# Polysketch attention and a multiplicative FFN in one kernel: another order of the same instructions from the 61st step on

## The chip, the cores and the metric

One core of a Trainium2 chip runs the whole kernel in one launch. The metric is device time in microseconds (us), the median of several runs. The engines are TensorE (PE in the profile, its weight loads PEld), VectorE (DVE), ScalarE (ACT) and GpSimd (POOL); SyncE (SP) issues nearly all DMAs. What a matmul computes lies in PSUM, in eight banks, until another engine reads it.

## The reference

The attention is linear: each q and k row of 32 numbers becomes 64 features, the outer product of two sketches of 8.

```
def phi(x):                                   # S1, S2: 8 x 32
    a = einsum('rd,bhsd->bhsr', S1, x)
    b = einsum('rd,bhsd->bhsr', S2, x)
    return outer(a, b) per row                # 64 features
q_p, k_p = phi(q), phi(k)                     # q, k, v: 4 x 4 x 1088 x 32
kv = einsum('bhsf,bhsd->bhfd', k_p, v);  z = sum over s of k_p
x = (q_p @ kv) / (q_p @ z + 1e-6)             # then heads side by side: 4352 x 128
out = (((x @ w1) * (x @ w2)) @ w3) @ w_out    # w1, w2: 128 x 1024, w3: 1024 x 1024, w_out: 1024 x 128
```

S1, S2 and the weights are float64 and come as 64-bit words, which the kernel turns into float32 itself; q, k and v are float32.

## The kernel before

The work is written as 1,179 small named steps (`@step("k0.gram1")`), each one to a few dozen instructions. A string of all the names, ORDER, says in which order they are emitted, and the main loop ties each engine's instructions into that order, so each engine runs its own part of the list strictly in sequence. An instruction waits for its operands and for the buffer that it writes; nothing behind it on its engine may overtake it. ORDER is thus a schedule written out by hand or by a planner, and three more tables belong to it: SLOTS says which buffer (SBUF tile or PSUM bank) each tile of a kind gets, POOL names the steps that run on GpSimd rather than on VectorE, and CPV the copies that run on VectorE rather than on ScalarE. WARM gives the lengths of twelve steps of filler matmuls of zeros (`warm0` to `warm11`, L255), which keep TensorE going while there is no work.

The loads of inputs (steps that end in `.load`) go through SP in the same order. Their instructions also carry a wait that the main loop adds: a bulk load is issued only when the fourth bulk load before it has landed (`UNDER_WAY = 4`; the small kr0 and kr1 loads don't count).

Names of steps: the letter and number ahead of the point is the part of the work.

- `k0` to `k3`: keys and values of batch 0 to 3. `k0.max`, `k0.g`, `k0.lead` and `k0.rest` split k into a leading part and a rest (kk, L651). `k0.gram0` to `k0.gram4` sum the products of k with itself (L659, small matmuls of 32 columns of the array). From the sum follow `k0.Gm`, `Gt`, `Ga`, `Gb` (L217, L201, L204, L865), on PE `k0.T0`, `T1` (L883 to L891), then `N0`, `N1` (L912), on VectorE `Nb` (L937), which together scale the denominators. `k0.tr0`, `tr1` transpose k (L685), `kT0`, `kT1` copy that (L690), `ab0`, `ab1` are the sketches (L702), `kp0`, `kp1` the features (L677), `kv0` to `kv3` and `kvr` the product with v (L769, L776), `kzt` and `kqt` transpose kv (L789, L805). `kr0`, `kr1` are the 64 last rows of each sequence, two batches at a time (`kr1.tr`, L819).
- `q0`, `q1`: the queries of batch 0, 512 tokens each. `q0.C0`, `q0.C1`, `q1.C0` (L1030) and `q0.A1`, `q1.A0` (L1057, L1110) are sketches on PE; on VectorE `sm`, `st`, `sh`, `sl` (L1137, L201, L204, L1157) and `Ct` (L1130) split and sum them, `p01`, `p2`, `p12` (L1180, L1184), `dn`, `de`, `rc` (L1189, L1194, L1198) give the reciprocal denominators, `phi0` and `phi1` the features (L1208). `pt0`, `pt1` transpose them (L1228, L1246), `x0`, `x1` multiply with kv (L1267), `xc` copies (L1274), and `xT0`, `xT1` (L1291) write xT, the input of the FFN. `q2`, `q3`, `q4`, `q6` and `qr` do the same for more tokens.
- `w0`, `w1` and so on: an eighth of w1 and w2 or w3 or w_out each; `.load` (L430) brings raw words, `.c`, `.m`, `.j`, `.a` turn them into float32 on ACT, VectorE and GpSimd (L466 is `.j`). `f0` to `f7` fold w3 and w_out into one matrix w3o (L528 to L538).
- `g0` to `g3`: the FFN of the first 2,048 tokens, 512 at a time, in eight chunks of d_ff: `g0.4a` and `g0.4b` are x·w1 and x·w2 of chunk 4 (L1799, L1809, 128x512 matmuls, the bulk of the kernel), `c` a copy (L1804), `m` the product (L1815), `o` the last matmul (L1835). `h4` and `h6` are batches 2 and 3, with seven products in place of eight (L1673, L1759), `gr` the 256 last tokens; `st` steps store.

The first 27 us hold the loads and the chain from k0 and q0 to the first xT; from there TensorE has FFN matmuls between which the steps of later batches are strewn. The last stretch is gr and the stores.

The emitting loop is this, and nothing in it changes:

```
for name in ORDER.split():
    n = len(traced)
    steps.pop(name)()
    if name.endswith(".load") and name not in ("s.load", "kr0.load", "kr1.load"):
        bulk += [i for i in traced[n:] if i.engine == nc.sync.engine]
for ins, ahead in zip(bulk[UNDER_WAY:], bulk):
    tc.add_manual_dep(ins, ahead.name, landed, reason="under way")
```

Of the kernel before, what the change touches and what calls it, by code (L numbers as in the profile page):

```python
# [82 lines left out]
q0.al k0.Nf q0.phi0 q0.phi1 q0.A1 q0.smy w1.m1 k1.max q0.sty q0.shy k0.kv3 k0.kv1 k0.kv2 q0.sly s.KS k0.kvr kr1.tr
k0.kvm w1.m0 kr1.kT q0.p01 q1.C0 q1.C1 q0.C1 k0.kzt k2.loadr q0.pt0 q0.C1t q0.scy q0.p2 k0.kz q0.pt1 k0.kvc kr1.ab
k0.kqt q0.p12 q0.dn q0.de q0.rc w1.j0 q0.pc0 q0.pc1 q0.x0 k1.kT0 q0.x1 q0.xs0 q0.xs1 q0.xt0 w1.a0 q1.A0 k2.load
w0.load k1.lead0 q0.xc0 q0.xc1 k0.kq w1.a1 k2.max q0.xt1 k1.ab q0.xT0 q0.xT1 g0.4a q1.load g0.5a q1.sm w0.m1 q1.st
q1.Ct g0.4c g0.4b q1.sh q1.sl k1.rest0 g0.7b w0.c1 g0.7a k1.abt w0.j1 k1.gram0 w0.c0 s.RC q1.scy k1.gram1 kh2.load
q1.sca q2.tr g0.5c q1.al q1.p01 q1.p2 k1.gram2 k1.gram3 kr1.abc k1.gram4 w6.load w0.m0 g0.6b w0.j0 g0.7c g0.7m k1.Gm
q1.p12 k1.Gc g0.0a w2.load w0.a1 q1.dn q1.de q1.rc q1.bs k1.Gt g0.3a k1.Ga k1.T0 k2.kT1 k1.Gb g0.3c q1.restT g0.2a
q1.phi k1.T1 q1.pt0 g0.4m w0.a0 q2.max q2.l2 g0.6a k1.Ta k2.lead0 k2.rest0 g0.1a g0.2c k1.Tc g0.5b q3.tr g0.5m k1.Tb  # L90
q1.pc0 q1.pt1 g0.1b w9.load k1.N0 s.AR q2.l1 q2.rm v3.zero q1.pc1 k1.N1 q1.x g0.6c g0.1c k1.Na k1.Nr k3.zero k2.gram0
g0.1m k2.gram1 k2.gram2 q3.max k2.gram3 g0.0c k2.kT0 k1.Nb q1.xT k2.gram4 q3.l2 k2.ab q2.A0 q2.C0 q2.C1 q3.l1 k1.kp0
v1.zero w9.c k2.abt g1.5a g1.5c g1.1a q2.Ct g1.7a q2.At q3.rm q3.A0 k0.Nr q2.sm q3.C0 q3.C1 k2.Gm v1.loadr q2.st w2.m
q2.sh g1.1c g1.2a k1.kp1 g0.6m q3.Ct g1.0a g1.7b k3.load v1.load g1.5b q3.At k2.Gt k3.loadr w2.c k2.Ga g0.0b w9.j
q2.sl g1.7c w6.c g1.6a k1.kv0 q3.sm k2.Gb w5.load q2.sc q2.al g1.0c k2.Gc g1.7m q2.p01 q3.st k1.kv2 k1.kv3 q3.sh w9.m
k1.kv1 k2.T0 k1.kvr q3.sl q2.p2 k2.T1 q2.p12 q2.dn q2.de g1.4a q2.rc k3.max g0.3b g0.0m g1.1b kh3.load g1.4c k2.Ta
g1.2b q3.sc g1.2c w5.c k2.Tc k1.kvc k1.kqt k1.kq g0.3m q3.p01 g1.6c g1.3a g1.5m g1.3b q2.bs q2.phi0 q2.pT0 g1.2m g1.3c
q2.x q2.load k2.N0 k2.Tb k3.lead0 w9.a1 k2.N1 g1.4b q3.al q3.p2 q3.p12 q2.xT0 g2.5a k3.kT1 g2.5c g2.6a q3.dn q3.de
k2.Na g1.3m g2.4a g2.3a w5.m g2.4b g2.6c k3.rest0 g1.0b k2.Nr q3.rc g1.1m g1.4m g1.6b k2.Nb g0.2b kr1.kp w6.j q4.tr
g2.4c g1.6m w7.load w7.c q3.bs q4.max q2.restT w6.m w5.j w2.j q4.l2 w3.load w9.a0 k3.gram0 k3.gram1 k3.gram2 q3.load  # L100
w7.j q3.phi0 k3.gram3 k3.gram4 g2.2a k3.Gc g2.1a g1.0m w2.a0 g2.6b g2.0a g2.4m g2.1c f6.t w6.a0 w4.load g2.3b w2.a1
g2.2b g2.2c g2.0c w6.a1 g2.1b q3.pT0 k3.Gm g0.2m k3.Gt k3.kT0 v3.load w7.m f6.m w5.a1 w5.a0 g2.3c k3.Ga k3.Gb g2.3m
w7.a0 g2.1m w3.m g2.6m q3.x k3.T0 k3.T1 f2.t w3.c w3.j w8.load g2.0b q3.xT0 g3.1a f6.o k3.Ta g3.0a g3.0b g2.7a g2.7b
q4.l1 w7.a1 q4.rm g3.0c g3.0m g2.5b v3.loadr g3.3a w4.c g2.0m g2.2m g3.1c g2.5m g2.7c g2.7m v2.zero g3.6a k3.Tb
v2.loadr k3.ab f4.t k3.Tc k3.abt w4.j g3.3c w3.a1 q4.A0 q4.C0 q4.C1 q4.At k3.N0 k3.N1 v2.load w3.a0 f0.t k2.kp1 f4.m
w4.m g3.6c q3.restT q6.tr g3.6b g3.6m q4.Ct q4.sm w10.load f0.m k2.kp0 f4.o g3.1b f0.o g3.1m qr.max q6.max k3.kp1
q4.st k2.kv0 w4.a1 k3.kp0 k2.kv3 k2.kv1 k2.kv2 k2.kvr q4.sh qr.l2 k3.kv0 k3.kv1 f3.t k2.kvc k3.kv3 k3.kv2 k3.Na w4.a0
qr.l1 qr.rm q4.sl q4.sc q4.al k3.kvr k3.kvc g3.4a q6.l2 g3.4c g3.4b q4.p01 k3.Nr g3.3b q6.l1 w8.c g3.5a k3.Nb g2.4o
g3.4m f1.t f3.m w10.c k3.kqt g3.5c w8.m g3.3m q4.p2 q6.rm k3.kq f1.m f1.o q6.A0 q6.C0 w10.j q6.C1 g3.1o f3.o w8.j
q4.p12 q6.At g3.2b w10.m q6.Ct q4.dn g3.7a q6.sm q6.st w8.a0 w10.a0 qr.A0 qr.C0 qr.C1 g3.0o g2.1o g3.7c w10.a1 g0.3o  # L110
qr.Ct qr.At q6.sh q4.de g1.4o q4.rc q4.bs g3.5b q4.na w8.a1 f2.m f2.o q6.sl q6.sc g2.3o f7.t qr.sm g3.5m q4.nb q4.nm
# [1823 lines left out]
```

## Time and profile before

| | before |
|---|---|
| median of 3 runs | 245.04 us (244.92 to 245.08) |
| span of the profiled execution | 244.1 us, 0.94 less than the median |
| mean granted TensorE clock | 0.998 |
| TensorE busy | 236.2 us, 97% |
| VectorE, GpSimd, ScalarE busy | 206.7, 161.9, 123.5 us |
| TensorE's share of the chain of work that ended last | 87% |

The profile is one execution. A row of the timeline has the start and length in us, the engine, the line, the operation, out<-in and how many are grouped; in brackets stands the idle time before it and what ended it. "Issue" means that the engine waited for nothing that the profile shows. A row of the stretches has, for each engine, its busy us and the number of its instructions, then the granted clock, the share of the DMA engines' time and GB/s. Rows of one DMA line end with the time from issue to landing. Where matmuls overlap, their lengths sum to more than the time that they take.

### The profile page before, as it was taken

What the parts mean: (1) busy time and instruction counts of PE and PEld (TensorE: products, weight loads), DVE (VectorE), ACT (ScalarE), POOL (GpSimd) and SP (SyncE); (2) the same over time, 40 slices, a digit from 0 to 9 for tenths busy, and PEclk for the clock granted to TensorE, in tenths of its full rate; (3) what the DMA queues carried; (4) which work ended last, traced back from release to release, by engine and by line L of the source; (5) the groups of instructions that cost most, each with busy time, mean ns of one, the idle gap of its engine ahead of it and who ended that gap; (6) DMA issues with size and microseconds to landing.
All of it is one profiled execution on the core that took longest, in us unless ns stands there. A gap on an engine that the chain in (4) does not pass through costs nothing.

```text
span 244.1 us, 6745 instructions
## 1 busy us (share of the span) xinstructions
PE 236.2 (97%) x2724; PEld 129.8 (53%) x2724; DVE 206.7 (85%) x421; ACT 123.5 (51%) x246; POOL 161.9 (66%) x203
## 2 busy tenths in 40 slices
...
GB/s 201 265 143 325 181 227 190 6 197 224 220 141 251 188 217 190 59 1 3 3 0 0 4 0 3 59 113 3 1 0 0 0 3 0 0 1 3 12 90 93
DMA packets 31935, 22.06 MB, mean 90 GB/s; under 512 B 21280, under 2 KB 26528, under 8 KB 31904
## 3 DMA queue, kind: packets, MB, share of 16 engines
...
q8 instruction: 21, 0.34, 0.6%
q10 hardware_dynamic: 544, 0.52, 0.6%
q14 instruction: 10, 0.08, 0.1%
...
## 4 chain that ended last, share of the span: by engine, by line
PE 87%; DMA 5%; ACT 2%; POOL 2%; DVE 1%; issue 1%; POOLq 0%; SPq 0%
PE b_ps L1809 12%; PE ps_o L1835 12%; PE ps_X L1673 11%; PE a_ps L1799 11%; PE ps_o L1759 10%; PE ps_w3o L534 6%; PE ps_Y L1673 6%; PE ps_Z L1673 3%; PE ps_g L659 2%; PE ps_x L1527 2%; PE ps_ac L1374 2%; DMA qh<-in_q_dram 2%; DMA k<-in_k_dram 2%; PE ps_or L1824 2%; POOL ph L1208 1%; PE idle_ps L255 1%
## 5 line engine op out<-in xcount | busy, mean ns | idle before, releaser
L1673 PE MATMUL ps_X<-xd,wv 64*128 64x512 f32 x112 | 36.3, 593 | 0.0
L1799 PE MATMUL a_ps<-xT,w 128*128 128x512 f32 (+1 forms) x80 | 36.1, 562 | 0.0
L1809 PE MATMUL b_ps<-xT,w 128*128 128x512 f32 (+1 forms) x80 | 35.6, 555 | 0.0
L1804 ACT COPY ffa<-a_ps 128x512 f32<-128x512 f32 (+1 forms) x38 | 20.1, 540 | 29.2 <-PE a_ps L1799 26.7
L1707 POOL TENSOR_TENSOR hc<-hc 128x512 f32<-128x512 f32 x16 | 20.7, 1304 | 15.7 <-DVE hc L1685 15.5
L1835 PE MATMUL ps_o<-ab,w3o 128*128 128x512 f32 x64 | 29.6, 600 | 0.0
L1680 ACT COPY hc<-ps_X 128x512 f32<-128x512 f32 x38 | 21.3, 590 | 16.1 <-PE ps_X L1673 12.9
L1815 DVE TENSOR_TENSOR ab<-ffa,b_ps 128x512 f32<-128x512 f32 (+1 forms) x40 | 23.9, 623 | 4.9 <-PE b_ps L1809 4.1
L501 POOL TENSOR_TENSOR w3c<-w3c,cv_m 128x512 int32<-128x512 int32 x16 | 21.2, 1344 | 4.2 <-DVE w3c L495 4.1
L1673 PEld LDWEIGHTS ps_X<-xd,wv 64*128 64x128 f32 x112 | 14.9, 186 | 13.1 <-issue 10.9
L1799 PEld LDWEIGHTS a_ps<-xT,w 128*128 128x128 f32 x80 | 14.1, 189 | 13.9 <-issue 8.8
L1809 PEld LDWEIGHTS b_ps<-xT,w 128*128 128x128 f32 x80 | 14.4, 190 | 13.1 <-issue 8.1
L1673 PE MATMUL ps_Y<-xd,wv 64*128 64x512 f32 x48 | 19.7, 594 | 0.0
L1835 PEld LDWEIGHTS ps_o<-ab,w3o 128*128 128x128 f32 x64 | 11.6, 190 | 13.4 <-issue 13.0
L534 PEld LDWEIGHTS ps_w3o<-wo,w3T 128*128 128x128 f32 x128 | 15.3, 192 | 2.4 <-issue 2.4
L534 PE MATMUL ps_w3o<-wo,w3T 128*128 128x128 f32 x128 | 15.7, 276 | 0.0
L1759 PE MATMUL ps_o<-hc,w3o 128*64 128x512 f32 x32 | 15.1, 595 | 0.0
L1759 PE MATMUL ps_o<-tt,ws 128*64 128x512 f32 x32 | 13.7, 594 | 0.0
L1680 ACT COPY hc<-ps_Y 128x512 f32<-128x512 f32 x14 | 8.1, 592 | 9.7 <-PE ps_Y L1673 6.6
L263 ACT ACTIVATE cv_c<-raw 128x1024 f32<-128x1024 f32 (+1 forms) x13 | 13.0, 1014 | 0.0
L1540 ACT COPY xd<-ps_x 64x256 f32<-64x256 f32 x24 | 8.8, 367 | 7.2 <-PE ps_o L1835 6.8
...
## 6 DMA issues: line engine op xcount, KB each, us to landing
...
```

The costliest lines, as they stand in the source:

```text
L263: act.activation(dst, hi.bitcast(F32), ACT.Prelu, scale=2.0 ** -112, alpha=-2.0 ** 32)
L501: pool.tensor_tensor(d, d, x["m"][:, i * 512:(i + 1) * 512], ALU.add)
L534: pe.matmul(t["o"], w3T[ko][:, c], wo[:, c], start=c == 0, stop=c == NC - 1)
L1673: pe.matmul(x[bank], stat(j, u)[:, i * 128:(i + 1) * 128], rows(j, u), start=new, stop=True, tile_position=(u * 64, 0), skip_group_check=True)
L1680: cp(n(y))(x[k], x[bank])
L1707: on(f"h{g}.{i}m{k}").tensor_mul(both[0][k], both[0][k], both[1][k])
L1759: pe.matmul(acc_o[bank][half[0]:half[1]], w(i), x(i), start=n == 1, stop=n == (2 if j == 3 else 4), tile_position=(0, half[0]), skip_group ...
L1799: pe.matmul(x["a"][:, :w], w_of(0, c), xT[g][:, c0:c0 + w], start=True, stop=True)
L1804: cp(f"g{g}.{c}{su}c")(x["s"][:, :w], x["a"][:, :w])
L1809: pe.matmul(x["b"][:, :w], w_of(1, c), xT[g][:, c0:c0 + w], start=True, stop=True)
L1815: dve.tensor_mul(ab_sb[g, c][:, c0:c0 + w], x["s"][:, :w], x["b"][:, :w])
L1835: pe.matmul(o_ps[g], w3o[:, c], ab_sb[g, c], start=n == 1, stop=n == NC)
```

## The change

Only the tables change: SLOTS, POOL, CPV, and ORDER from its 61st name on. The steps are the same 1,179, WARM too. POOL has 91 names in place of 90 (32 left, 33 came in), CPV 26 in place of 17. Of the names that matter in the first 50 us, `q0.phi0`, `q0.p2`, `q0.p12` and `k2.lead0` move to GpSimd, and `k0.kp1`, `k0.Nf`, `s.KS`, `q1.phi` and `k2.rest0` from it to VectorE. In all VectorE has 376 steps in place of 365, ScalarE 192 in place of 204, GpSimd 138 in place of 137.

```
 CPV = set("""
-    g0.0c g0.1c h4.1ac h4.1ad h6.1bc h6.2ad k0.kT1 k1.kvc k2.kT1 k2.kq k3.kT0 k3.kT1 k3.kq q0.xc0
-    q0.xc1 q6.xT0 q6.xT2
+    g0.3c g0.6c g1.2c g2.0c g2.2c g2.4c g2.5c g3.2c g3.3c gr.5c h4.0ac h4.0bd h4.2be h4.3bc h6.0bd
+    h6.1ac h6.2be k0.kT1 k1.kT0 k1.kvc kr1.kT q0.xc0 q1.pc1 q4.xT2 q4.xT3 q6.xT3
 """.split())
...
-k1.zero s.Pm warm5 q0.l1 q0.A0 warm6 kr0.ab k0.lead1 q0.rm q0.sma q0.sta warm7 k0.kT0 v0.load v0.loadr k1.load k0.ab1
-q0.sha k0.rest1 q0.C0 k0.gram1 k0.gram2 k0.gram3 k0.gram4 k0.ab0 k0.abc1 q1.max q0.C0t q0.sla q1.l2 k1.loadr s.Pp
...
+k1.zero s.Pm warm5 q0.l1 q0.A0 warm6 kr0.ab k0.lead1 q0.rm q0.sma k0.ab1 k0.gram1 q0.C0 k0.kT0 q0.sta kr1.load q0.sha
+s.KS k0.rest1 kr1.tr k0.gram2 warm7 k0.abc1 k0.ab0 q0.sla w1.c0 k0.kp1 kr1.kT q1.max w0.load kr0.abc k1.loadr q0.C0t
...
```

**SP, the loads behind the first weights** (raw tiles are a quarter of w1 and w2; k_264, v_146 and so on are tiles; L572, L593 and L609 load the last rows). Before:

```order
L430 DMA raw_211<-in_moe_w1_dram 128x512
L430 DMA raw_211<-in_moe_w2_dram 128x512
L582 DMA v_146<-in_v_dram 128x4x256
L593 DMA v_146<-in_v_dram 64x4x32
L560 DMA k_264<-in_k_dram 128x4x256
L572 DMA k_264<-in_k_dram 64x4x32
L609 DMA kr1_436<-in_k_dram 64x4x32 x2
```

And now:

```order
L430 DMA raw_211<-in_moe_w1_dram 128x512
L430 DMA raw_211<-in_moe_w2_dram 128x512
L609 DMA kr1_328<-in_k_dram 64x4x32 x2
L430 DMA raw_373<-in_moe_w1_dram 128x512
L430 DMA raw_373<-in_moe_w2_dram 128x512
L572 DMA k_264<-in_k_dram 64x4x32
L560 DMA k_264<-in_k_dram 128x4x256
L582 DMA v_146<-in_v_dram 128x4x256
L593 DMA v_146<-in_v_dram 64x4x32
```

The second pair of weights (step w0, raw_373) and k of batch 1 (k_264) stand ahead of v of batch 0 (v_146), which stood right behind the first pair.

**VectorE, the end of the chain to the first xT** (s_rc are the reciprocals, xc the copies, xT the FFN's input). Before:

```order
L1189 TENSOR_REDUCE s_d_620<-s_pr_561 128x2x16
L1194 SCALAR_TENSOR_TENSOR s_rc_622<-s_d_620 128x16
L1198 RECIPROCAL s_rc_622<-s_rc_622 128x16
L466 TENSOR_SCALAR w12_81<-cv_c_402 128x2x256
L1274 COPY xc_656<-ps_xt_629 128x256
L1274 COPY xc_656<-ps_xt_634 128x256
L1291 TENSOR_TENSOR xT_686<-xc_656,ps_xs_640 128x256
L1291 TENSOR_TENSOR xT_686<-xc_656,ps_xs_665 128x256
```

And now:

```order
L204 SCALAR_TENSOR_TENSOR s_hl_611<-s_g_540,s_t2_574 128x2x128
L466 TENSOR_SCALAR w12_81<-cv_c_516 128x2x256
L1130 STREAM_TRANSPOSE ay_C_642<-ps_c_578 128x384
L1189 TENSOR_REDUCE s_d_644<-s_pr_605 128x2x16
L466 TENSOR_SCALAR w12_81<-cv_c_364 128x2x256
L1194 SCALAR_TENSOR_TENSOR s_rc_653<-s_d_644 128x16
L1198 RECIPROCAL s_rc_653<-s_rc_653 128x16
L1157 TENSOR_TENSOR s_hl_611<-ps_a_525,s_hl_611 128x2x128
L690 COPY kT_665<-ps_kt_452 128x512
L1274 COPY xc_673<-ps_xt_660 128x256
L1291 TENSOR_TENSOR xT_683<-xc_673,ps_xs_680 128x256
L1291 TENSOR_TENSOR xT_683<-xc_673,ps_xs_687 128x256
```

Steps of q1 (s_hl_611, ay_C_642), a copy of k1's transposed keys (L690) and weight steps (L466) now stand among q0's last steps; one of the two copies L1274 went to ScalarE.

**TensorE, the gram of batch 2** (ps_g_959 before, ps_g_893 now, its sum in PSUM). Before, it follows q1's x and runs through its 72 matmuls to k2.ab (L727); its first rows:

```order
L912 MATMUL ps_N_920<-T_p_885,P2s_80 32x8 x8
L1297 MATMUL ps_x_944<-pT_906,kz0_605 64x512 x2
L659 MATMUL ps_g_959<-kk_891 32x64
L659 MATMUL ps_g_959<-k_439,kk_891 32x32
L659 MATMUL ps_g_959<-kk_891 32x64
```

Now it begins earlier and is broken off twice; the first break is this:

```order
L659 MATMUL ps_g_893<-k_650,kk_848 32x32
L883 MATMUL ps_T_936<-RS_71,G_a_930 32x32
L889 MATMUL ps_T_936<-RS_71,G_a_930 32x32
L890 MATMUL ps_T_936<-RS_71,G_c_910 32x32
L891 MATMUL ps_T_936<-RS_71,G_b_938 32x32
L659 MATMUL ps_g_893<-kk_848 32x64
L659 MATMUL ps_g_893<-k_650,kk_848 32x32
```

The second break, ahead of k2.gram3, is some 70 rows of other matmuls, three of them bulk ones of g1 at its end; k1.T0, k1.T1 stand in the first one.

More of the change, by code (lines that the diff above doesn't have):

```diff
@@ L83 @@
[L83 to L111, printed above, removed]
-g3.2a qr.st g3.2c g1.6o q4.nr q4.ne q4.nn q4.phi0 g0.2o q6.al k2.kqt f5.t g3.2m f5.m f5.o q4.phi1 q4.pT0 g3.7b g3.7m
```

132 lines of the change are left out of this document (81 added, 51 removed).

## The prediction

> **What bounds the kernel now.** I read the page first: who is busy, and where.
>
> ```profile
> PE 236.2 (97%) x2724; PEld 129.8 (53%) x2724; DVE 206.7 (85%) x421; ACT 123.5 (51%) x246; POOL 161.9 (66%) x203
> q8 instruction: 21, 0.34, 0.6%
> ```
>
> TensorE (PE) is busy for 236.2 of 244.1 us, so an order of the same matmuls can give at most the 7.9 us in which it is idle. The busy time in stretches says where those are (per engine: busy us, instructions; then the granted clock, the DMA share and GB/s).
>
> ```profile
> 5.00:10.00 5.00, 4.72 (x73) 3.72 (x70) 4.35 (x14) 3.86 (x14) 1.12 (x4) 1.00 0.93 218
> 10.00:15.00 5.00, 4.59 (x168) 4.25 (x160) 3.20 (x10) 4.56 (x9) 4.76 (x9) 1.00 0.88 256
> 20.00:25.00 5.00, 4.65 (x117) 3.86 (x116) 3.31 (x10) 3.05 (x11) 2.32 (x3) 1.00 0.91 292
> 45.00:50.00 5.00, 3.84 (x186) 2.74 (x175) 4.62 (x13) 2.26 (x3) 2.62 (x5) 1.00 0.05 10
> 240.00:245.00 5.00, 0.56 (x6) 0.37 (x4) 0.29 (x1) 0.27 (x1) 0.00 (x0) 0.82 0.32 66
> ```
>
> Two kinds of idle time: small pieces in the first 30 us, and one large piece at 45 to 50 us. What is lost at the end is the last tokens' chain through VectorE and the last store. The waits of PE and the timeline name the pieces.
>
> ```profile
> PE ps_g L659 <- issue: 1.6, 2, 1.2
> PE ps_kv L769 <- issue: 0.9, 1, 0.9
> PE ps_xs L1287 <- ACT xs L1280: 0.3, 1, 0.3
> PE ps_ph L1246 <- POOL ph L1208: 0.2, 1, 0.2
> ```
> ```profile
> 14.27 0.22 PE L659 MATMUL ps_g<-k,kk 128*32 128x32 f32 x1 [0.41 <-issue]
> 14.78 1.10 PE L702 MATMUL ps_ab<-RS,kT 128*128 128x64 f32 x8
> 18.06 0.26 PE L769 MATMUL ps_kv<-kp,v 128*32 128x64 f32 x3
> 20.35 0.69 PE L769 MATMUL ps_kv<-kp,v 128*32 128x64 f32 x34 [0.91 <-issue]
> 21.14 0.33 PE L819 MATMUL ps_krt<-ident,kr 128*128 128x128 f32 x1
> 27.42 1.10 PE L1799 MATMUL a_ps<-xT,w 128*128 128x512 f32 x2
> 46.98 0.19 PE L659 MATMUL ps_g<-k,kk 128*32 128x32 f32 x1 [1.16 <-issue]
> ```
>
> Three gaps, 0.41, 0.91 and 1.16 us, wait for nothing that the profile shows. All three lie inside runs of small matmuls (the gram, L659, and kv, L769). At 27.42 the first bulk matmul starts, a = x·w1 of the first 512 tokens; from there PE is full but for the last two kinds of gap. So the time is: when the bulk starts, plus the gaps behind it, plus a fixed amount of matmul work. I take the three gaps for the fetch of instructions: 2724 + 2724 instructions over 21 packets of queue q8 are 259 a packet, and one such packet is 16 KB. Counts over the same length of time before a gap and elsewhere:
>
> ```profile
> 11.00:13.90 2.90, 2.86 (x118) 2.66 (x115) 2.31 (x7) 2.83 (x7) 2.66 (x5) 1.00 1.00 281
> 16.60:19.50 2.90, 2.84 (x82) 2.07 (x80) 2.42 (x9) 2.73 (x8) 2.12 (x4) 1.00 0.77 256
> 43.00:45.90 2.90, 2.83 (x158) 1.88 (x149) 2.83 (x8) 2.32 (x6) 0.57 (x4) 1.00 0.02 6
> 31.50:34.50 3.00, 3.00 (x148) 2.27 (x147) 2.57 (x7) 2.49 (x6) 0.89 (x2) 1.00 0.94 221
> ```
>
> Before two of the gaps PE ran 233 and 307 instructions in 2.9 us, about a packet's worth; before the middle one 162. But 295 in 3 us went by without a gap, at 31.5. So density alone doesn't decide; where the run falls in its packet must do so too. The reading is likely, not sure.
>
> **The change part by part.** It moves steps from the 61st on; the matmuls stay the same. I go by the two ends of the sum: the bulk's start, and the gaps behind it.
>
> *The bulk's start.* It waits for xT of the first 512 tokens on VectorE (DVE), the end of this chain:
>
> ```profile
> 14.91 0.19 DVE L217 TENSOR_REDUCE G_g<-ps_g 128x1 f32<-128x32 f32 x1 [1.35 <-PE ps_g L659]
> 18.96 0.16 DVE L937 TENSOR_TENSOR RC<-RC,ps_Nr 128x8 f32<-128x8 f32 x1 [0.41 <-PE ps_Nr L912]
> 23.20 0.32 DVE L1068 STREAM_TRANSPOSE ay_C<-ps_cy 128x128 f32<-128x128 f32 x1 [1.38 <-PE ps_cy L1030]
> 26.48 0.79 DVE L1291 TENSOR_TENSOR xT<-xc,ps_xs 128x256 f32<-128x256 f32 x2
> ```
>
> From 14.91 to 27.27 DVE spends 12.36 us, of which 0.41 and 1.38 are waits: 10.57 of work. What the change takes out of that stretch and puts into it is priced by these rows:
>
> ```profile
> 19.64 0.78 DVE L1208 TENSOR_TENSOR ph<-s_al,s_bs 128x512 f32<-128x512 f32 x1
> 23.88 0.29 DVE L1180 TENSOR_TENSOR s_pr<-s_al,s_loy 128x128 f32<-128x128 f32 x1
> 15.69 0.42 DVE L466 TENSOR_SCALAR w<-cv_c 128x512 int32<-128x512 int32 x1
> 27.19 0.42 DVE L1137 TENSOR_REDUCE s_g<-ps_a 128x32 f32<-128x256 f32 x1
> 27.98 0.57 DVE L1130 STREAM_TRANSPOSE ay_C<-ps_c 128x384 f32<-128x384 f32 x1
> 6.71 0.67 DVE L690 COPY kT<-ps_kt 128x512 f32<-128x512 f32 x1
> ```
>
> Out: q0.phi0 (0.78) and q0.p2, q0.p12 (0.29 each) go to GpSimd, −1.36. In: a third weight step L466 (+0.42), the second half-batch's sm, st, sh, sl (four like L1137, 4 × 0.42) and Ct (0.57), the copy k1.kT0 (0.67) and a small step of the normaliser (about 0.2 by its neighbours): +3.54. Work 10.57 − 1.36 + 3.54 = 12.75. The two old waits are covered by this new work, so the stretch is only 0.4 longer if nothing new is waited for. It also begins later: k0.ab0 (L702, 1.10, some 0.1 of it overlapped), kr1.tr (0.33, likewise) and a filler stand ahead of the last gram matmuls now, and the 0.41 gap there goes; about +0.9 (0.7 to 1.1). DVE has k0.kp1 and the row transposes ahead of that point, which the old wait of 1.35 covers. Together the bulk would start 1.3 us later.
>
> *Late loads.* On SP the first weights' second quarter (w0, 1.05 MB) and k1 now stand ahead of v0.
>
> ```profile
> 5.52 0.43 SPq L582 DMA_DIRECT2D v<-in_v_dram  x1
> ```
> ```profile
> DMA to landing us min/median/max: 5.3/5.3/5.3
> ```
> ```profile
> DMA to landing us min/median/max: 7.2/7.2/7.2
> ```
>
> The first landing row is the w1 pair's, whose second half was issued at 5.1 and so landed at 10.4; the next is v0's: 5.52 + 7.2 = 12.7. So 0.52 MB behind w1 took 2.3 us. Here transfers issued together came in the order of issue. Now w0 (twice that), k1 and v0 follow w1: 10.4 + 4 × 2.3 = 19.6; at the best rate of a stretch (292 GB/s at 20 to 25 us) 2.1 MB take 7.2 us, 17.6. A bulk load is also held until the fourth before it has landed, so up to 20.9. k0.kv0 wants v0 on PE at 18.06 + about 0.5 (the gram before it is later by 0.9, of which fewer fillers make up some), and behind it on PE stands k0.N1, whose result the DVE chain needs (it already waited 0.41 for it). So the wait for v0 holds the bulk: 0 to 2.3 us, I take 0.7, since part of it falls while DVE still has other work. [...]
>
> Bulk start: 27.42 + 0.4 + 0.9 + 0.7 = 29.4, **+2.0 us** (+0.9 to +3.4).
>
> *The gaps behind it.* k2's gram is no longer one run: k1.T0, k1.T1, then bulk matmuls stand between its steps. If the gap at 46.98 is a fetch, it goes: **−1.16** (0 to −1.16). The wait of 0.2 for q1's ph (L1208 on GpSimd) goes, as that step now runs on DVE: **−0.2**.
>
> *Shape changes.* Going between matmuls of different array tiles costs PE a little:
>
> ```profile
> 49.17 2.77 PE a_ps L1799 x6
> 55.04 2.58 PE b_ps L1809 x6
> ```
>
> The same six, once beside narrower tiles and once among their like: 0.19 for a pair of changes. The changed program has two such pairs fewer: **−0.3** (0 to −0.4).
>
> *New waits.* k2.gram0 now follows soon after k2.rest0 on DVE, which stands behind q1.phi and a gram step there; g0.1a waits for a weight step on GpSimd behind k2.lead0, moved there. Neither shows in the trace of before. From zero to one bulk group of 1.7 us; I take **+0.4**, nearer zero, as DVE works ahead of PE by a few steps in this stretch.
>
> *The rest.* Behind 60 us PE is full in the trace and stays so with any order that keeps its operands ready. DVE has eleven steps more, at the 0.4 to 0.8 us of the rows above 4 to 9 us, on top of 85% busy, which can cost a little in the last stage of products; the chain of the last tokens at the end keeps its steps. I take nothing for both (−0.3 to +0.8).
>
> Sum: +2.0 − 1.16 − 0.2 − 0.3 + 0.4 = +0.7 (0.74). The profiled span is 244.1 and the median of the runs 245.04, 0.94 more; so 245.7.
>
> **The rivals.**
>
> *v0 lands in time* (faster). If the loads move at the higher rate, v0 and k1 are there by 18.5 us; the bulk starts 1.3 later, the gap of 1.16 goes, no new wait comes: +1.3 − 1.16 − 0.2 − 0.3 = −0.4, so 245.04 − 0.4 = 244.6; with 0.5 more from a chain of DVE that overlaps as well as it does now, 244.1. For it: 292 GB/s in one stretch. Against: 218 to 256 in the stretches that count. It decides at a landing of 18.5 us.
>
> *The loads are later still, and the gram waits* (slower). v0 at 20.9, k2.gram0 behind DVE by 1 us: 245.7 + 1.0 + 0.6 = 247.3. For it: the hold of four under way. Against: PE has several steps to fill with ahead of kv0's users.
>
> *The gaps are not fetches and stay* (the change doesn't do what it says). Then the 1.16 comes again at some place: 246.9. The row at 31.5 with 295 instructions and no gap speaks for it; the packet count, and that the waits show no engine, speak against it. [...]
>
> **How the numbers follow.** A measurement of this kernel can tell about 0.2%, 0.49 us, from no change: same is 244.55 to 245.53. The forecast's case, 0.42, spreads over 244.9 to 246.6: slower 0.22, same 0.15, faster 0.05. Loads in time 0.32: faster 0.24, same 0.08. Later still 0.14, gaps stay 0.12, both slower (0.01 of the last the same). That makes faster 0.29, same 0.24, slower 0.47. The range of 8 in 10 reaches from 244.0, the loads in time with a shorter chain (and 0.1 for the scatter of the runs), to 247.3, the late loads: the likeliest case's own range is 244.9 to 246.6.
>
> **What would show it.** Right: no wait "issue" over 0.5 us on PE behind the bulk's start; the first L1799 at 29 to 30 us; a wait of L769 or L912 for the DMA of v, or DVE waiting for ps_Nr by more than 0.41; the bulk's later start still there at the end. Wrong: the first L1799 at 28 or earlier, a gap of about 1 us in k2's gram, or a new wait over 1 us behind 50 us.

## The result and the profile after

The changed kernel takes 255.07 us (median, 254.3 to 256.9), the kernel before 244.98 us beside it (244.91 to 245.08): a ratio of 1.043, 95% interval 1.039 to 1.047. I had forecast 245.7 us and a range of 244.0 to 247.3; the sign was the likeliest one, the size was not in reach of the range. The profiled execution has a span of 255.1 us and a mean granted clock of 0.984, since the clock fell twice in it (0.72 and 0.84 in two of the stretches below); it is the slowest of the four (256.9). The kernel was run and profiled once more (e11 below): span 253.4 us, clock 0.997, the same waits. The clock's share is kept apart in what follows. Two executions of 607 us (e5) and 1341 us (the kernel before, beside e9 to e11) are in none of the times.

The page of the changed kernel, busy time of each engine:

```profile
PE 242.9 (95%) x2724; PEld 137.9 (54%) x2724; DVE 222.8 (87%) x435; ACT 115.6 (45%) x231; POOL 162.7 (64%) x204
```

The same 2,724 matmuls keep TensorE busy for 6.7 us more, and VectorE is busy for 16.1 us more with 14 more instructions, 1.2 us apiece. Both numbers should make a reader suspicious: a busy engine is not always an engine at work. The stretches and the waits of TensorE say where to look.

```profile
35.00:40.00 5.00, 3.67 (x11) 1.41 (x8) 4.97 (x6) 3.90 (x7) 4.79 (x2) 1.00 0.66 162
40.00:45.00 5.00, 4.25 (x60) 2.58 (x64) 4.89 (x8) 2.00 (x5) 2.07 (x3) 0.72 0.79 188
90.00:95.00 5.00, 3.17 (x79) 2.33 (x79) 4.25 (x7) 1.79 (x7) 2.12 (x2) 0.84 0.86 237
```
```profile
PE a_ps L1799 <- POOL w L470: 2.1, 1, 2.1
PE ps_x L1527 <- DVE ab L1815: 1.8, 1, 1.8
PE ps_g L659 <- issue: 1.1, 2, 0.7
```

Between 35 and 40 us VectorE is busy for 4.97 us with six instructions, GpSimd for 4.79 us with two. The timeline of GpSimd in the two places, then that of VectorE, and last the same two operations on VectorE in the kernel before:

```profile
35.21 4.25 POOL L214 TENSOR_SCALAR kk<-k,k_g 128x1152 f32<-128x1152 f32 x1 [1.28 <-PE ps_g L659]
39.43 1.27 POOL L470 TENSOR_TENSOR w<-w,cv_m 128x512 int32<-128x512 int32 x1
...
86.90 1.94 POOL L677 TENSOR_TENSOR kp<-kabt 128x1024 f32<-128x1024 f32 x1
88.79 0.20 POOL L577 MEMSET v<- 64x128 f32 x1
88.95 1.27 POOL L501 TENSOR_TENSOR w3c<-w3c,cv_m 128x512 int32<-128x512 int32 x1
90.19 1.94 POOL L677 TENSOR_TENSOR kp<-kabt 128x1024 f32<-128x1024 f32 x1
```
```profile
35.41 3.84 DVE L1204 TENSOR_TENSOR s_bs<-ay_C,s_rc 128x128 f32<-128x128 f32 x1
...
86.92 0.19 DVE L201 SCALAR_TENSOR_TENSOR G_t<-G_g,ps_g 128x32 f32<-128x32 f32 x1
87.02 1.88 DVE L1815 TENSOR_TENSOR ab<-ffa,b_ps 128x512 f32<-128x512 f32 x3
88.81 3.36 DVE L204 SCALAR_TENSOR_TENSOR G_a<-G_g,G_t 128x32 f32<-128x32 f32 x1
92.10 0.67 DVE L1815 TENSOR_TENSOR ab<-ffa,b_ps 128x512 f32<-128x512 f32 x1
```
```profile
15.36 0.19 DVE L204 SCALAR_TENSOR_TENSOR G_a<-G_g,G_t 128x32 f32<-128x32 f32 x1
39.51 0.86 DVE L214 TENSOR_SCALAR kk<-k,k_g 128x1152 f32<-128x1152 f32 x1
```

L204 on 128x32 took 0.19 us in the kernel before, at 15.36. Here it takes 3.36 and ends at 92.17, with GpSimd's kp (90.19 + 1.94 = 92.13); L1204 ends at 39.25, 0.2 us ahead of the end of GpSimd's L214 (39.46), and takes 0.29 us in e2 (35.78), where no GpSimd instruction runs beside it. The reading is that they are not slow but stand waiting while GpSimd runs, and that the profile counts this as busy. Both read two tiles of SBUF. L201 and the three products L1815 ahead of L204, which read one input from PSUM, run beside GpSimd's other kp (86.90 to 88.84) and take 0.19 us and 1.88 us for three, as in the kernel before (L201 at most 0.19 us, L1815 0.68 at the median). So this is the picture, which the experiments put to the test: k2.lead0 takes 4.25 us on GpSimd (0.86 on VectorE before), w0.a0 stands behind it and TensorE waits 2.08 us for w0.a0; and VectorE's k3.Ga stands through three GpSimd instructions in a row, the products behind it come 3.2 us late, and TensorE's q3.x, which needs their PSUM banks, waits 1.83 us.

How much of VectorE's 16.1 us is standing can be estimated from the traces: against the fastest instruction of the same operation, tiles and shape, its instructions take 14.0 us too long in all in the kernel before and 22.4 in the changed one. So about half, 8.4 us, is standing; the rest would be steps that came over.

The start of the bulk, and v0, of which the prediction spoke most:

```profile
L582 SPq DMA_DIRECT2D v<-in_v_dram x1: 374/374/374, 11.9 to 11.9; - x1
DMA to landing us min/median/max: 6.7/6.7/6.7
```
```profile
16.57 0.19 DVE L217 TENSOR_REDUCE G_g<-ps_g 128x1 f32<-128x32 f32 x1 [1.58 <-PE ps_g L659]
27.45 0.75 DVE L1291 TENSOR_TENSOR xT<-xc,ps_xs 128x256 f32<-128x256 f32 x2
```
```profile
19.39 0.43 PE L769 MATMUL ps_kv<-kp,v 128*32 128x64 f32 x16 [0.24 <-PE ps_kt L685]
28.35 3.67 PE L1799 MATMUL a_ps<-xT,w 128*128 128x512 f32 x8 [0.38 <-DVE xT L1291]
34.08 0.22 PE L659 MATMUL ps_g<-k,kk 128*32 128x32 f32 x1 [0.74 <-issue]
```

v0 landed at 11.9 + 6.7 = 18.6 and nobody waited for it. The bulk starts 0.9 us later than before. The gap of 1.16 us in k2's gram is gone; one of 0.74 has come in k1's gram.

To see where time is lost I add up, over TensorE's steps in order, how much longer each took (from its start to the next one's) than the same step in the kernel before. This is worked out from the starts in the traces; the columns are the places in the program, the times in the changed kernel.

| sum of the differences, us | first bulk | g0.1a (41 us) | g1.6a (57) | f3.m (105) | g0.5o (154) | end |
|---|---|---|---|---|---|---|
| changed kernel, e11 | +1.6 | +4.7 | +4.1 | +6.6 | +6.4 | +8.4 |
| e1: k2.lead0 on VectorE | +1.3 | +2.2 | +1.5 | +4.0 | +3.8 | +5.9 |
| e9: and k2.kp0, kp1 | +1.3 | +2.2 | +1.7 | +2.2 | +1.9 | +4.0 |

The last column can be read off directly: TensorE's last matmul starts at 248.72 us in e11 and at 240.28 in the kernel before.

### The profile page after: what moved, and what is told of

The parts are those of the page before. It is cut to its first block, busy times and chain, and to the rows that moved or that the text cites. A ratio compares the mean times of both kernels' runs of the same rounds, so it can differ in the third digit from the quotient of the medians.

```text
span 255.1 us, 6761 instructions
## 1 busy us (share of the span) xinstructions
PE 242.9 (95%) x2724; PEld 137.9 (54%) x2724; DVE 222.8 (87%) x435; ACT 115.6 (45%) x231; POOL 162.7 (64%) x204
## 3 DMA queue, kind: packets, MB, share of 16 engines
HBM read 19.40 MB, written 2.23 MB: 85 GB/s over the span
## 4 chain that ended last, share of the span: by engine, by line
PE 82%; DVE 6%; POOL 4%; DMA 4%; issue 1%; ACT 1%; POOLq 0%; DVEq 0%; SPq 0%; ACTq 0%
PE ps_X L1673 11%; PE ps_o L1835 11%; PE ps_o L1759 10%; PE a_ps L1799 10%; PE b_ps L1809 9%; PE ps_Y L1673 5%; PE ps_w3o L534 5%; PE ps_Z L1673 3%; PE idle_ps L255 3%; PE ps_g L659 3%; DMA qh<-in_q_dram 2%; PE ps_ac L1374 2%; PE ps_x L1527 2%; POOL kk L214 2%; PE ps_or L1824 2%; DVE G_a L204 1%
## 5 line engine op out<-in xcount | busy, mean ns | idle before, releaser
L1673 PE MATMUL ps_X<-xd,wv 64*128 64x512 f32 x112 | 39.9, 597 | 0.0
L1809 PE MATMUL b_ps<-xT,w 128*128 128x512 f32 (+1 forms) x80 | 37.3, 573 | 0.0
L1804 ACT COPY ffa<-a_ps 128x512 f32<-128x512 f32 (+1 forms) x30 | 15.5, 536 | 37.3 <-PE a_ps L1799 36.2
L1815 DVE TENSOR_TENSOR ab<-ffa,b_ps 128x512 f32<-128x512 f32 (+1 forms) x40 | 24.0, 620 | 3.8 <-ACT ffa L1804 2.3
L1707 POOL TENSOR_TENSOR hc<-hc 128x512 f32<-128x512 f32 x16 | 21.9, 1379 | 7.3 <-DVE hc L1685 7.2
L1673 PEld LDWEIGHTS ps_X<-xd,wv 64*128 64x128 f32 x112 | 17.8, 186 | 10.6 <-issue 5.6
L1673 PE MATMUL ps_Y<-xd,wv 64*128 64x512 f32 x48 | 22.4, 600 | 0.0
L1809 PEld LDWEIGHTS b_ps<-xT,w 128*128 128x128 f32 x80 | 14.6, 196 | 13.0 <-issue 10.1
L1509 POOL TENSOR_TENSOR ph<-s_al,s_bs 128x1024 f32<-128x1024 f32 (+1 forms) x6 | 11.2, 1868 | 5.2 <-DVE s_bs L1459 3.6
L677 POOL TENSOR_TENSOR kp<-kabt 128x1024 f32<-128x1024 f32 x5 | 9.7, 1943 | 6.3 <-DVE w3T L528 6.3
L1540 ACT COPY xd<-ps_x 64x256 f32<-64x256 f32 x20 | 7.3, 366 | 13.2 <-PE ps_x L1527 12.9
L1759 PE MATMUL ps_o<-hc,ws 128*64 128x512 f32 x32 | 12.2, 594 | 0.0
```

The source lines that it names most:

```text
L1673: pe.matmul(x[bank], stat(j, u)[:, i * 128:(i + 1) * 128], rows(j, u), start=new, stop=True, tile_position=(u * 64, 0), skip_group_check=True)
L1707: on(f"h{g}.{i}m{k}").tensor_mul(both[0][k], both[0][k], both[1][k])
L1759: pe.matmul(acc_o[bank][half[0]:half[1]], w(i), x(i), start=n == 1, stop=n == (2 if j == 3 else 4), tile_position=(0, half[0]), skip_group ...
L1804: cp(f"g{g}.{c}{su}c")(x["s"][:, :w], x["a"][:, :w])
L1809: pe.matmul(x["b"][:, :w], w_of(1, c), xT[g][:, c0:c0 + w], start=True, stop=True)
L1815: dve.tensor_mul(ab_sb[g, c][:, c0:c0 + w], x["s"][:, :w], x["b"][:, :w])
```

## The experiments

Spans stand beside the medians, since single executions of one kernel lie up to 3.6 us apart here (e2), often with the granted clock (0.993 in the shortest of e2, 0.984 in the longest). Each ratio is to the kernel before on the same chip.

**e1, k2.lead0 back on VectorE**, the changed kernel otherwise.

```
 POOL = set("""
-    ... k2.kp0 k2.kp1 k2.lead0 k3.Nr ...
+    ... k2.kp0 k2.kp1 k3.Nr ...
```

> The changed kernel, with k2.lead0 back on VectorE (as before the change). Theory A, GpSimd's step of 4.25 us (L214, 35.21 to 39.46) causes both the wait of TensorE for w0.a0 (2.08 us) and the 3.84 us that VectorE's q1.bs (L1204) took beside it: both go, L1204 takes about 0.3 us, and the time falls by 2.1 us or more, 3.3 us where the lower clock at 40 to 46 us goes with it: 251.5 to 252.8 us. Theory B, VectorE has too much work in this stretch and TensorE would be held all the same: the wait of L1799 goes but another of 1 us or more comes within 10 us, and the time falls by less than 1 us: over 254 us.

253.41 us (252.58 to 254.51), ratio 1.0325 [1.0271, 1.0378]; span 250.8 at clock 0.998. VectorE's rows:

```profile
35.47 0.78 DVE L213 TENSOR_SCALAR kk<-k,k_g 128x1152 f32<-128x1152 f32 x1
36.16 1.38 DVE L1203 TENSOR_TENSOR s_bs<-ay_C,s_rc 128x128 f32<-128x128 f32 x1
```

The step takes 0.78 us in place of 4.25, the wait of 2.08 us is gone and no other over 0.7 comes until 88 us: theory A by the mechanism. The median is 0.6 us above the range that I had given, as two of the four executions ran at a clock of 0.99 (the other two, 252.58 and 252.65, lie inside it); the span is 2.6 us less than that of e11. L1203 (the line numbers are one less) still stands 1.1 us (1.38 less the 0.29 of e2) beside GpSimd's w0.a0 (1.26 us at 36.13), longer than I had said.

**e2, w0.a0 ahead of k2.lead0**, both on GpSimd.

```
-g0.7b q2.max k2.lead0 q2.l2 q1.bs k1.Gm g0.0c w0.a0 q3.l2 g0.3a
+g0.7b q2.max w0.a0 k2.lead0 q2.l2 q1.bs k1.Gm g0.0c q3.l2 g0.3a
```

> The changed kernel, with w0.a0 put ahead of k2.lead0, both still on GpSimd. If only the place in GpSimd's queue matters (theory A1), TensorE's wait of 2.08 us goes and the time falls by 2 us or more, as in the run with k2.lead0 on VectorE. If what GpSimd's long step does to VectorE matters too (theory A2), L1204 still takes over 3 us, q1.phi and what follows come as late as now, TensorE waits for them 1 us or more between 36 and 46 us, and less than 1.5 us is gained.

258.03 us (254.64 to 258.25), ratio 1.0465 [1.0392, 1.0538]. TensorE's waits, and VectorE and GpSimd:

```profile
PE ps_ph L1246 <- DVE G_t L201: 2.2, 1, 2.2
```
```profile
38.96 0.71 DVE L720 STREAM_TRANSPOSE kT<-kh 128x512 f32<-128x512 f32 x1 [2.79 <-DMA kh<-in_k_dram]
39.60 3.53 DVE L1208 TENSOR_TENSOR ph<-s_al,s_bs 128x1024 f32<-128x1024 f32 x1
```
```profile
38.15 4.25 POOL L214 TENSOR_SCALAR kk<-k,k_g 128x1152 f32<-128x1152 f32 x1
```

The weight step is out of the queue's way and nothing is gained: GpSimd's 4.25 us now hold VectorE's q1.phi (3.53 us, 1.18 in e1), for which TensorE waits 2.2 us. L1204 itself is free (0.29 us at 35.78), not over 3 us as A2 had said: VectorE then waited 2.79 us for a load, which let q1.phi fall beside the long step. So the long step on GpSimd held another two-tile instruction of VectorE when that came beside it, 3.53 us in place of 1.18 (A2), and its place in GpSimd's queue is not the whole of the cost; by how much the late load added to it this run doesn't say.

**e3, GpSimd idle beside k3.Ga**: w7.a1 and k2.kp1 behind w3.a1.

```
-... k3.T0 k3.T1 w7.a1 k3.Ta q4.l1 f6.o g2.7b q3.xT0 k2.kp1 w3.j ... q4.A0 w3.a1 w8.load
+... k3.T0 k3.T1 k3.Ta q4.l1 f6.o g2.7b q3.xT0 w3.j ... q4.A0 w3.a1 w7.a1 k2.kp1 w8.load
```

> The changed kernel, with GpSimd's steps w7.a1 and k2.kp1 put behind w3.a1, so that GpSimd is idle from about 89 us until 96 us. Theory A: VectorE's k3.Ga (L204, 3.36 us at 88.81) stood waiting for GpSimd's steps and takes 0.2 to 1 us now, g2.4m comes 2 to 3 us sooner, TensorE's wait of 1.83 us in q3.x goes, and the time falls by 1.8 us or more: 251 to 253 us. Theory B, VectorE's load holds TensorE: the wait in q3.x shrinks by less than 0.5 us or comes again behind it; over 254 us.

253.98 us (253.84 to 254.41), ratio 1.0336 [1.0301, 1.037].

```profile
87.49 0.18 DVE L205 SCALAR_TENSOR_TENSOR G_a<-G_g,G_t 128x32 f32<-128x32 f32 x1
```
```profile
94.55 2.94 POOL L678 TENSOR_TENSOR kp<-kabt 128x1024 f32<-128x1024 f32 x1
```
```profile
PE ps_ac L1366 <- ACT ffa L1805: 1.4, 1, 1.4
```

L205 takes 0.18 us: the block is gone, and so is the wait in q3.x. But another wait of 1.45 us stands at 96.7: kp, moved late, keeps its input's buffer, ScalarE's copy L1805 starts at 97.52 when kp ends at 97.49, and the PSUM banks behind it come free late. My edit made that wait, so this run shows the block and not its price, and its time lies between the two forecasts.

**e4, the kernel before with its gram split**: k2.gram3 and gram4 behind g1.7a.

```
-... k2.gram1 k2.gram2 q3.max k2.gram3 g0.0c k2.kT0 k1.Nb q1.xT k2.gram4 q3.l2 k2.ab ... g1.7a q2.At
+... k2.gram1 k2.gram2 q3.max g0.0c k2.kT0 k1.Nb q1.xT q3.l2 k2.ab ... g1.7a k2.gram3 k2.gram4 q2.At
```

> The kernel before, with k2.gram3 and k2.gram4 behind g1.7a, so that three bulk matmuls and other work stand inside the gram; nothing else is changed. If the gap of 1.16 us in k2's gram is a fetch of instructions that a run of small matmuls outruns, it goes: 243.8 to 244.2 us. If it is something else that the gram meets at that place or time, a gap of about that size comes in the gram's second part or beside it: 244.8 to 245.3 us.

247.12 us (246.24 to 248.23), ratio 1.0052 [1.0027, 1.0076]: slower, by 0.5%, and in neither of the two ranges.

```profile
PE a_ps L1799 <- DVE ab L1815: 1.2, 1, 1.2
PE ps_ab L727 <- DVE RC L936: 1.2, 1, 1.2
```
```profile
52.38 2.23 DVE L204 SCALAR_TENSOR_TENSOR s_hl<-s_g,s_t 128x256 f32<-128x256 f32 x1
```

The gap in the gram is gone, and at the same place k2.ab waits 1.2 us for VectorE's k1.Nb (L936), which frees its PSUM bank. Part of that wait is made by the edit, since a third of the gram no longer stands ahead of k2.ab; the rest stood behind the gap before. The second wait of 1.2 us, at 55.3, is another block: L204 takes 2.23 us beside GpSimd's kp (52.38 to 54.32), where it took 0.42 in the kernel before. The gram's later end moved kp there. So the run shows that the gap goes, and not what it is worth.

**e5, both collisions undone**: as e1, and k2.kp0, kp1 behind w3.a1 on GpSimd.

```
-... w6.a0 k3.Gb k2.kp0 w3.c q3.x ... q3.xT0 k2.kp1 w3.j ... q4.A0 w3.a1 w8.load
+... w6.a0 k3.Gb w3.c q3.x ... q3.xT0 w3.j ... q4.A0 w3.a1 k2.kp0 k2.kp1 w8.load
```

> The changed kernel with k2.lead0 back on VectorE, and k2.kp0 and k2.kp1 on GpSimd behind w3.a1, so that GpSimd is idle while VectorE does k3.Ga; w7.a1 stays where it is. If the two collisions of VectorE and GpSimd are what cost the time up to 97 us (theory A), both waits of TensorE are gone and nothing over 1 us comes in their place: the span is 1.8 us less than the 250.8 of the run with k2.lead0 alone, 249.0, and the time about 250.8 us. If VectorE or the copies bound the kernel there anyway (theory B), a wait of 1 us or more stands behind 88 us again, and the span is over 250 us.

253.28 to 256.21 us in three executions; the profiled one took 607 us, so there is no profile to read. No gain over e1, as theory B had said. The two runs made on its base, e7 and e8, point to why: k3.Ga is free there (0.18 and 0.19 us), but TensorE waits 2.1 us at 95 to 98 us for ScalarE's L1804 behind the late kp, as in e3.

**e6, the kernel before with k2.lead0 on GpSimd**, one name more in POOL.

```
-    ... k2.kp0 k2.kp1 k2.rest0 ...
+    ... k2.kp0 k2.kp1 k2.lead0 k2.rest0 ...
```

> The kernel before with k2.lead0 on GpSimd, the one name of the table that the change moved there in this stretch. Theory A: the step takes 4.2 us there in place of 0.86, VectorE's steps that read two tiles of SBUF stand still for 1 to 3 us beside it, and the kernel is 2 to 4 us slower: 247 to 249 us. Theory B: only the new order has no room for it, and the kernel before hides it: under 246 us.

247.25 us (246.69 to 248.55), ratio 1.009 [1.0054, 1.0126].

```profile
39.72 4.25 POOL L213 TENSOR_SCALAR kk<-k,k_g 128x1152 f32<-128x1152 f32 x1
44.05 2.73 POOL L650 TENSOR_TENSOR kk<-k,kk 128x1152 f32<-128x1152 f32 x1
```
```profile
PE ps_g L658 <- POOL kk L650: 2.4, 1, 2.4
```

The one name costs 1.9 us there too, as theory A had said, of which the lower clock of three of the four executions is a part: the one at full clock took 246.69. The way is another one. TensorE's gram waits 2.4 us for k2.rest0, which follows on GpSimd, and this wait stands in the place of the gap of 1.16. Beside the 4.25 us themselves VectorE hardly stood: only L382, at 1.16 us in place of 0.82, as until its last 0.4 us no other two-tile instruction came there; one of 1.61 us (L203, 0.17 in the kernel before) stood beside k2.rest0.

**e7, seven copies of the products' stage from VectorE to ScalarE**, on e5.

```
 CPV = set("""
-    ... gr.5c h4.0ac h4.0bd h4.2be h4.3bc h6.0bd h6.1ac h6.2be k0.kT1 ...
+    ... gr.5c k0.kT1 ...
```

> As the run with both collisions undone, and the seven copies of the products' stage that VectorE does (h4.0ac and so on) go to ScalarE, which is 20 to 60% busy there. From about 160 us to the end the changed kernel loses 1.8 us against the one before. If VectorE's greater load in that stage is the cause, 1.2 to 1.8 us come back; if the cause is the pairs of VectorE and GpSimd steps that block each other (L1707, L1727), whatever the load, less than 0.6 us comes back.

255.41 us (254.31 to 255.59), ratio 1.0405 [1.0368, 1.0441]. From g0.5o on the sum grows by 3.3 us, in e8 on the same base by 2.0: 1.3 us lost, none won. TensorE waits for ScalarE's copies there:

```profile
PE ps_X L1673 <- ACT hc L1680: 0.5, 1, 0.5
```

So ScalarE can't take the copies without holding TensorE itself, and nothing speaks for VectorE's load as the cause of the loss; that it has no part in it the run doesn't show.

**e8, q1.sl and k1.kT0 behind q0.xT1**, k1.ab behind the first four bulk matmuls, on e5.

```
-... q0.x0 q1.sl k2.load k1.kT0 q0.xs0 ... q0.xT1 q3.tr q1.sca k1.lead0 k1.ab q1.al ... g0.4a q1.p2
+... q0.x0 k2.load q0.xs0 ... q0.xT1 q1.sl k1.kT0 q3.tr q1.sca k1.lead0 q1.al ... g0.4a k1.ab q1.p2
```

> As the run with both collisions undone, and q1.sl and k1.kT0 behind q0.xT1 on VectorE, with k1.ab behind the first four bulk matmuls on TensorE. VectorE's two steps (1.1 us) are out of the chain to the first xT: the first L1799 starts 1.0 to 1.1 us sooner, at about 27.4 us. If the later start of the bulk is passed on to the end, the time falls by about 1 us; if VectorE bounds the stretch from 30 to 55 us, as the split gram of the kernel before suggests, most of it is lost to a wait for VectorE between 33 and 50 us.

253.93 us (253.21 to 253.94), ratio 1.0347 [1.0323, 1.0372]. The bulk starts later, not sooner:

```profile
29.13 1.85 PE L1799 MATMUL a_ps<-xT,w 128*128 128x512 f32 x2 [1.61 <-DVE kT L690]
```

The first a_ps uses the PSUM bank that k1.kT0 empties, so the copy stood where it had to. That run cannot say what the two steps are worth.

**e9, k2.lead0, k2.kp0 and k2.kp1 on VectorE**, the changed kernel otherwise: three names less in POOL, the order as it was.

```
-    ... k2.Nr k2.kp0 k2.kp1 k2.lead0 k3.Nr ...
+    ... k2.Nr k3.Nr ...
```

> The changed kernel with k2.lead0 and also k2.kp0 and k2.kp1 on VectorE: GpSimd is idle while VectorE does k3.Ga, and the tile that kp reads comes free no later than in the changed kernel, unlike where kp was put behind w3.a1 and ScalarE's copies (L1804) had to wait for that tile's buffer. Theory A, the block of VectorE by GpSimd (3.36 us) makes TensorE's wait of 1.8 us in q3.x: L204 takes 0.2 to 0.3 us, the wait goes, and the span is 1.5 to 2.3 us under the 250.8 of the run with k2.lead0 alone: 248.5 to 249.3 us, though VectorE has 2.4 us more to do. Theory B, VectorE's load is what holds TensorE: the 2.4 us more make another wait of 1 us or more between 88 and 110 us, and the span is 250 us or more.

250.72 us (250.29 to 252.2), ratio 1.0192 [1.0128, 1.0255]; span 248.9 at clock 0.998.

```profile
86.05 0.19 DVE L203 SCALAR_TENSOR_TENSOR G_a<-G_g,G_t 128x32 f32<-128x32 f32 x1
86.15 0.68 DVE L1814 TENSOR_TENSOR ab<-ffa,b_ps 128x512 f32<-128x512 f32 x1
86.75 0.19 DVE L864 TENSOR_TENSOR G_b<-ps_g,G_a 128x32 f32<-128x32 f32 x1
86.85 1.22 DVE L676 TENSOR_TENSOR kp<-kabt 128x1024 f32<-128x1024 f32 x1
```

With 2.4 us more work VectorE is through sooner, L203 takes 0.19 us, and no wait comes at 85 to 110 us. Three names of 91 are worth 4.4 us of the loss (8.4 to 4.0 in the table).

**e10, the products' stage with the GpSimd steps of before**, on e1: 13 names of h4 and h6 out of POOL, 11 in.

```
-    h4.0m11 h4.1T1 h4.1T3 h4.1T4 h4.2T3 h4.3T4 h4.3m22 h4.s1 h6.0T1 h6.0T3 h6.0T4 h6.2m22 h6.s3
+    h4.0T2 h4.0T3 h4.2m12 h4.2m22 h4.s2 h4.s4 h6.0m11 h6.1T3 h6.2T1 h6.2T4 h6.s1
```

> The changed kernel with k2.lead0 on VectorE, and in the products' stage (h4, h6) the same 31 steps on GpSimd as before the change, in the changed order. Giving ScalarE seven more copies cost 1.3 us there, so VectorE's load was not what held TensorE. If the choice of steps for GpSimd is the cause of the 1.8 us that the changed kernel loses from 150 us to the end, 1 us or more of it comes back (span under 250 us); if it is the new order of that stage, or how the two fall on each other by chance, the loss stays between 1.3 and 4 us.

266.72 us (266.02 to 267.34), ratio 1.0828 [1.0774, 1.0881].

```profile
PE ps_o L1758 <- POOL tt L1726: 2.7, 1, 2.7
```

From g0.5o on 14 us are lost, far over both forecasts; the wait shown is the longest. The order and the choice of engine in that stage go together: the new order with the old choice is far worse than either kernel as it was. Whether the new choice costs the 2 us there is not answered by it.

**e11, the changed kernel again.**

> The changed kernel once more, as it is, beside the two others on one chip. 252.5 to 253.6 us of span where TensorE's clock stays at full, up to 255.1 where it drops behind the waits of 2.08 and 1.83 us; L1204 and L204 stand still for over 3 us again in both cases if GpSimd's steps block them, since nothing of it is chance.

255.28 us (253.8 to 255.88), ratio 1.0353 [1.0298, 1.0408]; the kernel before took 244.89 to 246.88 us on that chip. The waits of 2.08 and 1.82 us are there again, the clock is 0.997 and the span 253.4. Both blocks repeat: 3.57 us for L1204 and 3.36 for k3.Ga. A third one shows that the profile of the result lacks:

```profile
PE ps_T L883 <- DVE G_a L204: 0.7, 1, 0.7
```

Here k0.Ga (L204 at 16.88) takes 0.79 us, beside q0.phi0 (L1208), which the change moved to GpSimd and which runs from 16.56 to 17.63. In the other profile it runs from 16.07 to 17.14, half a microsecond sooner, and L204, at 17.02, takes 0.19. The same program can meet a block or miss it.

**e12, the kernel before with q0.C1 ahead of the kv matmuls**, as the changed kernel has it.

```
-... k0.kv3 k0.kv1 k0.kv2 q0.sly s.KS k0.kvr kr1.tr ... q1.C0 q1.C1 q0.C1 k0.kzt
+... k0.kv3 q0.C1 k0.kv1 k0.kv2 q0.sly s.KS k0.kvr kr1.tr ... q1.C0 q1.C1 k0.kzt
```

> The kernel before with q0.C1 behind k0.kv3 on TensorE, ahead of the other kv matmuls, as the changed kernel has it; nothing else. VectorE's wait of 1.38 us for ps_cy (L1068 at 23.20) falls to under 0.3 us, and the first L1799 starts 0.4 to 1.0 us sooner than at 27.42. If TensorE from there on is what sets the time, that comes back at the end: 244.0 to 244.6 us, the only version here under the kernel before. If VectorE bounds the stretch from 36 to 55 us, it is lost to a longer wait there, and the time stays within 0.3 us of the kernel before.

245.42 us (244.63 to 246.85) against 245.67 (244.9 to 246.6), ratio 0.999 [0.9971, 1.0009].

```profile
21.81 0.30 DVE L1068 STREAM_TRANSPOSE ay_C<-ps_cy 128x128 f32<-128x128 f32 x1
```
```profile
26.75 1.96 PE L1799 MATMUL a_ps<-xT,w 128*128 128x512 f32 x4
```
```profile
PE ps_g L659 <- issue: 1.2, 1, 1.2
```

VectorE's wait for ps_cy is gone, the bulk starts 0.67 us sooner, and the sum over TensorE's steps in the profiles keeps the 0.7 to the end. The gap in the gram comes 0.67 us sooner with it, unchanged. The interval of the runs holds both 0.7 us and nothing, so that this version beats the kernel before is not shown: by the times the second forecast holds, by the profile the first.

## Why the prediction was wrong

**What held.** That the bulk starts later (that a shift of its start is kept to the end, e12's profile shows, its times don't). That the gap in k2's gram goes. That waits, not matmuls, make the difference, and that the sign is most likely slower. One of its signs of being wrong came, a new wait over 1 us behind 50 us (1.83, ended at 92.8).

**Late loads, +0.7: nothing.** v0 landed at 18.6, within the bounds of 17.6 to 20.9 that I had, and TensorE came to kv only at 19.4. The chain on VectorE began 1.66 us later than before (16.57), not 0.9, but took 11.6 us from there to xT's end (28.2), less than the 12.4 of before and not 0.4 more, as it met no long wait. Sum for the start: +0.9 (28.35) and +1.4 (28.8) in the two profiles, where +2.0 and a range of +0.9 to +3.4 had been said; the two differ by the block of k0.Ga.

**The gap, −1.16: it bought less than it was.** The prediction took the gap in k2's gram for time that comes back whole. What was queued next on VectorE was not asked:

```profile
46.58 0.12 DVE L936 TENSOR_TENSOR RC<-ps_N,RC 128x8 f32<-128x8 f32 x1
```

This step frees the PSUM bank of k2.ab, which began at 47.53 in the kernel before. Without the gap the gram would have ended 1.16 us sooner, at 46.37, and k2.ab would have waited for L936 until 46.70: some 0.8 us could come back, an estimate from these rows. In the changed kernel the sum falls by 0.6 to 0.7 between 41 and 57 us. And a gap came elsewhere: k1's gram got one of 0.74 (0.46 in e11). That small gaps come and go with the order is shown (1.16 us gone, 0.74 come); that they are fetches of instructions was an estimate from the packet count, and no run shows it.

**New waits, +0.4 with at most 1.7: the step that failed.** The prediction named the very place, "g0.1a waits for a weight step on GpSimd behind k2.lead0, moved there", and gave it no price of its own. The price of k2.lead0 on GpSimd was not in the trace of before (no TENSOR_SCALAR of that size ran there), and the bound taken was one bulk group, which had nothing to do with it. The nearest rows would have been one operation on both engines: ph (L1208, 128x512) takes 1.51 us on GpSimd and 0.78 on VectorE in the trace of before, so twice 0.86, 1.7 us. It was 4.25, five times, so that even the better bound would have been too low. The one TENSOR_SCALAR that GpSimd did run there could have warned: L409 took 0.89 us for 32x32. The 2.08 us of wait follow from the 4.25 (e1); in place of +0.4, what hangs on k2.lead0 cost 2.5 us. The other wait that the prediction named, k2.gram0 for k2.rest0, came with 0.63 us in e11.

**The rest, taken at nothing with −0.3 to +0.8: the larger failure.** The sum added up durations on each engine as if they did not touch each other. Two engines did, and the sum had no term for it. The trace of before showed it to whoever looked at the outliers of one form:

```profile
81.27 1.30 DVE L204 SCALAR_TENSOR_TENSOR G_a<-G_g,G_t 128x32 f32<-128x32 f32 x1
...
87.12 1.19 DVE L204 SCALAR_TENSOR_TENSOR T_p<-T_g,T_t 32x32 f32<-32x32 f32 x1
```

The first took 1.30 us for what takes 0.19, beside GpSimd's w3c steps, and ended (82.57) when one of them did (82.52); it cost TensorE nothing there. The second is of the same kind, 1.19 us for 0.18, ended at 88.31 with a w3c step at 88.27. The later traces show it again: L1204 took 3.84 us beside GpSimd's 4.25, and 1.38 in e1 beside 1.26, for 0.29 in e2. At 88.81 VectorE stood through w3c (1.27 us) and on through GpSimd's kp at 90.19 though it had been waiting since before that began, 3.36 us in all. How the two engines come to block each other no trace shows. e9 against e1 shows what this block costs: 1.9 us (5.9 to 4.0 in the table, 250.8 to 248.9 in the spans).

**What stays open.** From g0.5o to the end the changed kernel loses 2 us more. It is made of some twenty pieces of 0.1 to 0.5 us, the largest 0.3 to 0.5 behind products whose VectorE steps (L1707, L1727) stand beside GpSimd's for 0.4 to 1.1 us. That these cause them was only argued: five instructions of VectorE stand there for over 0.4 us each in e11 and one in the kernel before, but e7 only speaks against VectorE's load, and e10 does not tell the rest apart. Also open are 0.9 us between the first bulk matmul and 41 us that e1 and e9 keep, about half of it the gap in k1's gram.

**The sum, as measured (e11):** start and chain +1.6 (filler matmuls moved later in it), k2.lead0 and what hangs on it about +2.5 (4.7 less the 2.2 that e1 keeps), rest up to 41 us +0.6, gaps up to 57 us −0.6, from there to f3.m +2.5 (1.9 of it the block of k3.Ga), elsewhere −0.2, last stage +2.0: 8.4. Behind TensorE's last matmul 0.8 us more are lost, which the prediction had at nothing too ("the chain of the last tokens at the end keeps its steps"): it is followed by 4.37 us in place of 3.55, as SyncE is still issuing the stores ahead (L1556, until 250.07) when the last result is ready at 249.29. Together, but for rounding, that is the 9.3 us between the spans 253.4 and 244.1. The medians lie 10.1 us apart, since the profiled execution of the kernel before was longer than its median one: times here lie about 1.8 us above their spans, and 245.04 only 0.94 above 244.1. Where the clock falls behind the two waits, 1.7 us come on top (255.1 against 253.4).
